# Gate and value products issued back to back in four 32-row strips, and a pipelined prologue

## The chip, the cores and the metric

The kernel runs on one core of a Trainium2 chip. The metric is the device time of one execution in microseconds (us). The kernel before takes 1056.0 us (median of two runs, 1054.63 to 1057.37).

In the profile, PE is the matmul engine, PEld its weight loads, DVE the vector engine, ACT the scalar engine, POOL the GpSimd engine and SP the engine that queues most transfers. "L267" is line 267 of the kernel that the trace belongs to. The granted clock is the share of full speed at which PE was allowed to run, by the profile. PSUM is the memory that PE writes its products to. A strip is the band of rows of PE's array that a product occupies, here 32 or 64 of 128.

## The reference, cut to what matters

Two stages follow each other. The first is attention through 32 inducing points, the second a gated feed-forward layer:

```
h    = softmax(scale * I @ x.T) @ x          # per batch, 32 x 128
x2   = softmax(scale * x @ h.T) @ h          # per token, rank 32
g, v = x2 @ w_gate, x2 @ w_val               # 128 -> 1536
out  = x2 + sigmoid(x2 @ w_res) * ((gelu(g) * v) @ w_out)
```

There are 4 batches of 12416 tokens of 128 channels. Because x2 is a mix of the 32 rows of h, the kernel never forms x2 for the wide products: it multiplies h by w_gate and w_val once per batch (`hg`, `hv`, 1536 columns) and mixes the results with the softmax weights of each token (`rt`). The contraction of the gate and value products is thus only 32 long. `h`, `hg`, `hv` and `rt` are stored four times, in partitions 0-31, 32-63, 64-95 and 96-127.

## The kernel before

A group is 512 tokens (the last group of a batch has 128). A group has six slots of 256 hidden columns, each of two 128-column chunks. Gate and value chunks use two copies at once, 64 rows, with 0.5 in the weights to make up for the doubling:

```python
def slot_mms(gi, si, weights):
    ...
    for c in [i // 2 + (i % 2) * half for i in range(2 * half)]:
        if c < cn:
            r = slice(64, 128) if c >= half else slice(0, 64)
            pe.matmul(v[:, c * tw:(c + 1) * tw],
                      weights[b][r, (c0 + c) * P:(c0 + c + 1) * P], rt[r, :],
                      start=True, stop=True)
```

The loop over slots (`prev` is the group before, whose output products `mms` fill PE's time; `gate` and `residual` are two small mixes that ACT reads with a tanh and a copy; `end` is the last multiply of a group on DVE):

```python
for p in range(nper):
    if nxt[0] < ngrp:
        gate_slot(*nxt)                 # gate products and GELU of slot p+1
    if prev and p == nper - 1:
        ...  prev.end()
    if prev:
        prev.mms(quota // 2)            # five output products
    value_mms(gi, p)                    # into the buffer that the GELU of p has read
    value_mul(gi, p)                    # DVE: u = gelu * value
    if prev:
        prev.mms(quota - quota // 2)    # five more
    if prev and p == 0:
        prev.gate()
    elif prev and p == 2:
        prev.residual()
    for f in todo.pop((g, p), []):      # work for the next batch
        f()
```

There are three PSUM buffers of 1024 columns for gate/value, shared with the scores, one for the output products and one for mixes. Work for the next batch (loading x, scores, exponentials, accumulation, `hg` and `hv`) is spread over the groups. Three bursts of exponentials per batch interrupt the plain groups. The prologue makes h of batch 0: 13 tiles of x, each transposed, copied, scored and accumulated in turn; then weights are cast, seven softmax tiles are normalised on POOL and transposed by DMA, and last w_out is loaded and scaled on DVE.

The softmax here doesn't subtract the row's maximum and nothing guards it: scores larger than these inputs give would overflow.

Of the kernel before, what the change touches and what calls it, by code (L numbers as in the profile page):

```python
# [9 lines left out]
FP32 = mybir.dt.float32  # L10
# [3 lines left out]
AC = mybir.ActivationFunctionType  # L14
# [4 lines left out]
def kernel(  # L19
# [171 lines left out]
    def first_layer(dst, w, b, c0, c1, eng):  # L191
        bank = wide_bank()
        for c in range(c0, c1, TOK):
            e = min(c + TOK, c1)
            pe.matmul(bank[:, c - c0:e - c0], ht_t[b], w[:, c:e], start=True, stop=True)
        if eng is act:
            act.activation(dst[:, c0:c1], bank[:, :c1 - c0], AC.Copy, bias=0.0, scale=0.5)
        else:
            ve.tensor_scalar(dst[:, c0:c1], bank[:, :c1 - c0], 0.5, None, op0=AL.mult)

    def res_layer(b):
        bank = misc_bank()
        pe.matmul(bank[:, :P], ht_t[b], wR, start=True, stop=True)
        hr = p_h.tile([P, P], FP16, name="hr", tag="hr")
        hr_t[b] = hr
        act.activation(hr, bank[:, :P], AC.Copy, bias=0.0, scale=1.0)

    def exp_b(b, j0, j1):
        n = (j1 - j0) * M
# [43 lines left out]

    gv_t, ge_t, u_t = {}, {}, {}

    def slot_mms(gi, si, weights):
        b, k, j0, nb, slots = groups[gi]
        tw = nb * P
        c0, cn = slots[si]
        rt = rt_t[b, k][:, j0:j0 + nb, :].rearrange("p j t -> p (j t)")  # L260
        v = gv_t[gi, si]
        half = TOK // tw

        for c in [i // 2 + (i % 2) * half for i in range(2 * half)]:
            if c < cn:
                r = slice(64, 128) if c >= half else slice(0, 64)
                pe.matmul(v[:, c * tw:(c + 1) * tw],  # L267
                          weights[b][r, (c0 + c) * P:(c0 + c + 1) * P], rt[r, :],
                          start=True, stop=True)

    def gate_slot(gi, si):
        n = groups[gi][4][si][1] * groups[gi][3] * P
        gv_t[gi, si] = wide_bank()
        slot_mms(gi, si, hg_t)
        ge = p_ge.tile([P, 2 * TOK], FP32, name="ge", tag="ge")
        act.activation(ge[:, :n], gv_t[gi, si][:, :n], AC.Gelu, bias=0.0, scale=1.0)  # L276
        ge_t[gi, si] = ge

    def value_mms(gi, si):
        slot_mms(gi, si, hv_t)  # L280

    def value_mul(gi, si):
        n = groups[gi][4][si][1] * groups[gi][3] * P
# [4 lines left out]
    class Last:  # L288
# [17 lines left out]
                pe.matmul(self.ffn[:, k, :], u_t[self.gi, si][:, o:o + P], wO[:, fc, :],  # L306
                          start=(fc == 0), stop=(fc == FCH - 1))

        def mix(self, h, r):
            bank = misc_bank()  # L310
            for k in range(self.nk):
                pe.matmul(bank[:, k * P:(k + 1) * P],  # L312
                          rt_t[self.b, self.k][r, self.j0 + k, :],
                          h[r, :], start=True, stop=True)
            return bank

        def gate(self):
            bank = self.mix(hr_t[self.b], slice(0, M))
            self.th = p_fin.tile([P, TOK], FP32, name="th", tag="th")
            act.activation(self.th[:, :self.tw], bank[:, :self.tw], AC.Tanh,  # L320
                           bias=0.0, scale=0.5)

        def residual(self):
            bank = self.mix(ha_t[self.b], slice(0, 2 * M))
            self.at = p_fin.tile([P, TOK], FP32, name="at", tag="at")
            act.activation(self.at[:, :self.tw], bank[:, :self.tw], AC.Copy,  # L326
                           bias=0.0, scale=1.0)
# [42 lines left out]
    pieces = []  # L370
    for dst, src in ((wG, moe_w_gate), (wV, moe_w_val), (wR, moe_w_res)):
        n = dst.shape[1]
        for o in range(0, n, PRE * P):
            w = min(PRE * P, n - o)
            pieces.append((dst[:, o:o + w], src[:, o:o + w], w))

    def weight_in(i):
        dst, src, w = pieces[i]
        wf = p_x.tile([P, PRE, P], FP32, name="xf", tag="xf")
        xf_t["w", i] = wf  # L380
        sy.dma_start(wf.rearrange("p k c -> p (k c)")[:, :w], src)

    def weight_cast(i, eng):
        dst, src, w = pieces[i]
        eng.tensor_copy(dst, xf_t.pop(("w", i)).rearrange("p k c -> p (k c)")[:, :w])


    for k in range(ntile):
        convert(0, k, ve, po if k % 2 else ve)
        if k + 3 < ntile:  # L390
            fetch(0, k + 3)
        elif k + 3 - ntile < len(pieces):
            weight_in(k + 3 - ntile)
        turn_pe(0, k)
        n0, w = blocks_of(k)
        exp_a(0, n0, n0 + w)
        if k:
            p0, pw = blocks_of(k - 1)
            accumulate(0, p0, p0 + pw, k == 1, False)
    n0, w = blocks_of(ntile - 1)  # L400
    for i in range(len(pieces)):
        weight_cast(i, po)
        if i + 3 < len(pieces):
            weight_in(i + 3)
    accumulate(0, n0, n0 + w, False, True)
    finish_h(0)
    turn_h(0)
    half = PRE // 2
    e2 = exp_b(0, 0, PRE)
    norm_b(0, 0, PRE, e2)  # L410
    weights_b(0, 0, 0, half)
    weights_b(0, 0, half, PRE)
    for i, c0 in enumerate(range(0, F, 2 * TOK)):
        c1 = min(c0 + 2 * TOK, F)
        first_layer(hg_t[0], wG, 0, c0, c1, act)
        first_layer(hv_t[0], wV, 0, c0, c1, ve)
    res_layer(0)
    for j0 in range(PRE, 8 * PRE, 4 * PRE):
        j1 = min(j0 + 4 * PRE, 8 * PRE)
        e2 = exp_b(0, j0, j1)  # L420
        norm_b(0, j0, j1, e2)
        for k in range(j0 // PRE, j1 // PRE):
            weights_b(0, k)
    for o in range(0, FCH, PRE):
        w = min(PRE, FCH - o)
        wf = p_x.tile([P, PRE, P], FP32, name="xf", tag="xf")
        sy.dma_start(wf[:, :w, :], moe_w_out.rearrange("(f p) d -> p f d", p=P)[:, o:o + w, :])
        ve.tensor_scalar(wO[:, o:o + w, :], wf[:, :w, :], 0.5, None, op0=AL.mult)
    warm = ps_f.tile([P, TOK // P, P], FP32, name="ffn", tag="ffn")
    for i in range(14):  # L430
        pe.matmul(warm.rearrange("p k c -> p (k c)"), wG[:, :P], wG[:, :TOK],
                  start=True, stop=True)

# [3 lines left out]
    def plan(b):  # L437
# [3 lines left out]
            todo.setdefault((g, p), []).append(f)  # L441

        nb = b + 1
        if nb < B:
            for k in range(ntile):
                g = k if k < 10 else k + 1
                at(g, 1, lambda k=k: fetch(nb, k))
                at(g + 1, 1, lambda k=k: convert(nb, k, po, po))
                at(g + 1, 4, lambda k=k: turn(nb, k))
# [13 lines left out]
        if nb < B:  # L463
            for h in range(2):
                for i in range(2):
                    j0 = (4 * h + 2 * i) * PRE
                    at(11 + h, 3 + i, lambda j0=j0, i=i: accumulate(
                        nb, j0, j0 + 2 * PRE, i == 0, i == 1))

            def burst_two():  # L470
                exp_a(nb, nfull, nblk - 1)
                exp_a(nb, nblk - 1, nblk)
            at(16, 3, burst_two)
            at(17, 3, lambda: accumulate(nb, nfull, nfull + 2 * PRE, True, False))
            at(17, 4, lambda: accumulate(nb, nfull + 2 * PRE, nblk, False, True))
            at(18, 1, lambda: finish_h(nb))
            at(18, 3, lambda: turn_h(nb))
            spots = [(18, 4), (18, 5), (19, 1), (19, 3), (19, 4)]
            for c0 in range(0, F, 2 * TOK):
                c1 = min(c0 + 2 * TOK, F)  # L480
                at(*spots.pop(0), lambda c0=c0, c1=c1: first_layer(hg_t[nb], wG, nb, c0, c1, act))
                at(*spots.pop(0), lambda c0=c0, c1=c1: first_layer(hv_t[nb], wV, nb, c0, c1, act))
            at(*spots.pop(0), lambda: res_layer(nb))

            def burst_three():
                for j0, j1 in ((0, 4 * PRE), (4 * PRE, 8 * PRE)):
                    norm_b(nb, j0, j1, exp_b(nb, j0, j1))
            at(20, 3, burst_three)
            for i in range(8):
                at(20 + (i + 2) // 3, 2 * ((i + 2) % 3), lambda i=i: weights_b(nb, i))  # L490
        return todo
# [4 lines left out]
    for gi in range(ngrp):  # L496
# [7 lines left out]
        for p in range(nper):  # L504
            nxt = (gi, p + 1) if p + 1 < nper else (gi + 1, 0)
            if nxt[0] < ngrp:
                gate_slot(*nxt)
            if prev and p == nper - 1:
                prev.mms(len(prev.todo))
                if nper == 2:  # L510
                    prev.residual()
                prev.end()
            if prev:
                prev.mms(quota // 2)
            value_mms(gi, p)
            value_mul(gi, p)
            if prev:
                prev.mms(quota - quota // 2)
            if prev and p == 0:
                prev.gate()  # L520
            elif prev and p == 2:
# [40 lines left out]
```

## Time and profile before

| | before |
|---|---|
| time, median | 1056.0 us |
| span of the profiled run | 1045.0 us |
| PE / DVE / ACT busy | 86 / 77 / 73% |
| mean granted clock of PE | 0.948 |
| interval between group ends, plain groups | 8.95 us |
| first multiply of the slots / first group end | 77.99 / 95.27 us |

The "group end" is the start of the last DVE instruction of a group (L331 in the kernel before, L333 in the changed one). Intervals between these starts show a period far better than shares of the span. The row of the page that gives the clock granted to PE in 40 equal slices of the span, in tenths:

```profile
PEclk9967998899989999899989999899998999999999
```

The 6 and 7 at the left are the idle start; the 8s lie behind the bursts.

### The profile page before, as it was taken

To read this page: it belongs to the slowest core of one execution; us is meant where nothing else is said; L and a number is where in the kernel's file an instruction comes from. 1 tells how busy PE (TensorE), PEld (TensorE's weight loads), DVE (VectorE), ACT (ScalarE), POOL (GpSimd) and SP (SyncE) were. 2 spreads that over 40 slices of the span, in tenths; PEclk is the share of its full clock that TensorE was granted. 3 is DMA by queue.
4 is the path that set the end of the run, shared out by engine and by line. 5 is a ranking of instruction groups with operands and counts; after the bars stand their busy time and mean duration, and the time that the engine had idled before them with its cause. 6 is when DMAs were issued, how large, how long until landed. Compare 5 with 4: busy or idle time off the path is not lost.

```text
span 1045.0 us, 23183 instructions
## 1 busy us (share of the span) xinstructions
PE 896.1 (86%) x9536; PEld 487.5 (47%) x9536; DVE 804.8 (77%) x776; ACT 768.0 (73%) x879; POOL 353.1 (34%) x308
## 2 busy tenths in 40 slices
PE   4618998999789899898889999898889899889997
PEld 3404444545445444444445444455444444444444
DVE  6317887787678888687777888678777888788886
ACT  4416788677867778778777877778777778887775
POOL 3452553621162554351134444441125111141111
PEclk9967998899989999899989999899998999999999
DMA  6362452510043444440022545340014000030000
GB/s 212 103 125 72 122 121 63 123 45 22 22 92 95 114 115 106 69 90 32 21 61 72 121 117 114 78 115 33 21 34 100 27 29 31 32 73 31 32 30 35
DMA packets 114186, 77.04 MB, mean 74 GB/s; under 512 B 92416, under 2 KB 95136, under 8 KB 114080
## 3 DMA queue, kind: packets, MB, share of 16 engines
q1 hardware_dynamic: 114080, 75.57, 28.7%
q8 instruction: 74, 1.21, 0.5%
q14 instruction: 32, 0.26, 0.1%
HBM read 27.87 MB, written 25.43 MB: 51 GB/s over the span
## 4 chain that ended last, share of the span: by engine, by line
PE 73%; DVE 11%; ACT 7%; issue 5%; DMA 2%; POOL 1%; SPq 0%; DVEq 0%; POOLq 0%; ACTq 0%
PE ffn L306 34%; PE gv L267 30%; PE ms L312 6%; DVE th L331 5%; DVE u L285 5%; ACT ge L276 2%; ACT xt L123 1%; PE gv L122 1%; PE gv L132 1%; DMA rt<-a 1%; ACT e L213 1%; DVE z L220 1%; PE ms L153 1%; ACT e L140 1%; POOL a L234 1%
## 5 line engine op out<-in xcount | busy, mean ns | idle before, releaser
L285 DVE TENSOR_TENSOR u<-ge,gv 128x1024 bf16<-128x1024 f32 x584 | 701.7, 1215 | 171.1 <-PE gv L267 167.9
L276 ACT ACTIVATE ge<-gv 128x1024 f32<-128x1024 f32 x584 | 593.0, 1019 | 112.4 <-PE gv L267 98.2
L306 PE MATMUL ffn<-wO,u 128*128 128x128 bf16 x4656 | 438.5, 226 | 21.4 <-DVE th L331 19.6
L306 PEld LDWEIGHTS <-u 128*128 128x128 bf16 x4656 | 276.9, 99 | 252.6 <-issue 241.2
L334 POOL TENSOR_TENSOR at<-at,th 128x512 f32<-128x512 f32 (+1 forms) x100 | 123.9, 1239 | 598.2 <-ACT ge L276 312.8
L267 PE MATMUL gv<-rt,hg 64*128 64x512 f16 (+1 forms) x1200 | 250.9, 392 | 84.2 <-DVE u L285 70.9
L267 PE MATMUL gv<-rt,hv 64*128 64x512 f16 (+1 forms) x1200 | 235.6, 392 | 9.1 <-ACT ge L276 9.1
L267 PEld LDWEIGHTS <-hg 64*128 64x128 bf16 x1200 | 77.6, 94 | 161.1 <-issue 124.5
L320 ACT ACTIVATE th<-ms 128x512 f32<-128x512 f32 (+1 forms) x100 | 58.5, 585 | 84.1 <-PE ms L312 81.8
L234 POOL TENSOR_TENSOR a<-e,z 128x1024 f16<-128x1024 f32 (+2 forms) x53 | 92.2, 1753 | 44.2 <-DVE z L221 32.0
L267 PEld LDWEIGHTS <-hv 64*128 64x128 bf16 x1200 | 66.2, 93 | 73.8 <-issue 20.8
L107 POOL TENSOR_TENSOR lo<-xf,hi 128x1024 f16<-128x1024 f32 (+1 forms) x45 | 90.8, 2018 | 19.4 <-DVE hi L105 19.0
L326 ACT ACTIVATE at<-ms 128x512 f32<-128x512 f32 (+1 forms) x100 | 58.4, 584 | 41.5 <-PE ms L312 41.5
L331 DVE SCALAR_TENSOR_TENSOR th<-th,ffn 128x512 f32<-128x512 f32 (+1 forms) x100 | 66.4, 664 | 6.1 <-ACT th L320 4.7
L312 PEld LDWEIGHTS <-rt 32*128 32x128 f16 (+1 forms) x776 | 44.7, 95 | 24.8 <-issue 5.6
L312 PE MATMUL ms<-ha,rt 64*128 64x128 f16 x388 | 39.3, 221 | 2.4 <-ACT th L320 2.4
L105 POOL CAST hi<-xf 128x1024 f16<-128x1024 f32 (+1 forms) x39 | 38.2, 981 | 8.4 <-DMA xf<-in_x_dram 8.4
L312 PE MATMUL ms<-hr,rt 32*128 32x128 f16 x388 | 40.0, 223 | 0.5 <-ACT at L326 0.5
L132 PEld LDWEIGHTS <-xt 128*128 128x128 f16 x776 | 22.8, 98 | 24.7 <-ACT xt L123 17.1
L132 PE MATMUL gv<-I1T,xt 128*128 128x32 f16 x388 | 13.7, 182 | 18.7 <-ACT xt L123 13.8
L220 DVE TENSOR_REDUCE z<-e 128x32 f32<-128x1024 f32 (+3 forms) x17 | 15.1, 887 | 13.8 <-ACT e L213 13.8
L123 ACT ACTIVATE xt<-gv 128x1024 f16<-128x1024 f16 (+1 forms) x13 | 12.6, 967 | 16.4 <-PE gv L122 16.4
(58 smaller groups left out, 237.2 us busy)
## 6 DMA issues: line engine op xcount, KB each, us to landing
xf<-in_x_dram SPq DMA_DIRECT2D x48, 512.0 KB, 4.2
out_dram<-at SPq DMA_DIRECT2D x96, 256.0 KB, 2.1
rt<-a SPq DMA_TRANSPOSE x53, 3.1
xt<-hi SPq DMA_TRANSPOSE x39, 4.5
xf<-in_moe_w_gate_dram SPq DMA_DIRECT2D x1, 512.0 KB, 3.4
xf<-in_moe_w_val_dram SPq DMA_DIRECT2D x1, 512.0 KB, 3.8
xf<-in_moe_w_out_dram SPq DMA_DIRECT2D x1, 512.0 KB, 4.5
xf<-in_x_dram SPq DMA_DIRECT2D x4, 64.0 KB, 2.1
```

The source lines that it names most:

```text
L107: e_lo.tensor_tensor(lo[:, :w, :P], xf[:, :w, :], hi[:, :w, :], AL.subtract)
L132: pe.matmul(bank[:, (j - j0) * M:(j - j0 + 1) * M], xt_t[b, k][:, jj, :], rows, start=True, stop=True)
L234: po.tensor_tensor(a2[:, :n], ev[:, o:o + n, :].unsqueeze(2).to_broadcast([P, n, Q, M]), z[:, 1, o:o + n].unsqueeze(2).unsqueeze(3).to_bro ...
L267: pe.matmul(v[:, c * tw:(c + 1) * tw], weights[b][r, (c0 + c) * P:(c0 + c + 1) * P], rt[r, :], start=True, stop=True)
L276: act.activation(ge[:, :n], gv_t[gi, si][:, :n], AC.Gelu, bias=0.0, scale=1.0)
L285: ve.tensor_tensor(u[:, :n], ge_t.pop((gi, si))[:, :n], gv_t.pop((gi, si))[:, :n], AL.mult)
L306: pe.matmul(self.ffn[:, k, :], u_t[self.gi, si][:, o:o + P], wO[:, fc, :], start=(fc == 0), stop=(fc == FCH - 1))
L312: pe.matmul(bank[:, k * P:(k + 1) * P], rt_t[self.b, self.k][r, self.j0 + k, :], h[r, :], start=True, stop=True)
L320: act.activation(self.th[:, :self.tw], bank[:, :self.tw], AC.Tanh, bias=0.0, scale=0.5)
L326: act.activation(self.at[:, :self.tw], bank[:, :self.tw], AC.Copy, bias=0.0, scale=1.0)
L331: ve.scalar_tensor_tensor(self.th[:, :tw], self.th[:, :tw], 1.0, self.ffn.rearrange("p k c -> p (k c)")[:, :tw], AL.add, AL.mult)
L334: po.tensor_tensor(self.at[:, :tw], self.at[:, :tw], self.th[:, :tw], AL.add)
```

## The change

Its intent: put all four chunks of a slot (two gate, two value) in a 32-row strip of their own, so that they can run at once; issue them together, so that PE changes between kinds of product less often; and take the serial start apart.

```diff
-                r = slice(64, 128) if c >= half else slice(0, 64)
+                r = slice((q0 + (c >= half)) * M, (q0 + (c >= half) + 1) * M)
...
-        slot_mms(gi, si, hg_t)
+        slot_mms(gi, si, hg_t, 0)
...
-        slot_mms(gi, si, hv_t)
+        slot_mms(gi, si, hv_t, 2)
...
             if nxt[0] < ngrp:
                 gate_slot(*nxt)
+            value_mms(gi, p)
             if prev and p == nper - 1:
                 ...  prev.end()
-            if prev:
-                prev.mms(quota // 2)
-            value_mms(gi, p)
             value_mul(gi, p)
             if prev:
-                prev.mms(quota - quota // 2)
+                prev.mms(quota)
```

The factor 0.5 in `hg`/`hv` becomes 1.0, and `hr` gets a low part (one small DVE subtraction per batch), so that both mixes use 64 rows. The prologue is pipelined over three tiles, its conversions are all on DVE, and weights come through ACT's queue during the first pass:

```diff
+    for k in range(ntile + 2):
+        if k < ntile:
+            convert(0, k, ve, ve)
+            ...  turn_pe(0, k)
+        if 2 <= k and k % 2 == 0 and k // 2 - 1 < len(pieces):
+            weight_in(k // 2 - 1)
+        ...
+        if 1 <= k <= ntile:
+            ...  exp_a(0, n0, n0 + w)
+        if k >= 2:
+            ...  accumulate(0, n0, n0 + w, k == 2, k == ntile + 1)
...
+        if b == 0:
+            for i in range(1, 8):
+                at((i - 1) // 2, 2 + 3 * ((i - 1) % 2), lambda i=i: weights_b(0, i))
```

Last, half of the first layer of the next batch moves into the third burst, read by DVE instead of ACT:

```diff
-            spots = [(18, 4), (18, 5), (19, 1), (19, 3), (19, 4)]
-            ...  five pieces of first layer and res_layer, on act
             def burst_three():
-                for j0, j1 in ((0, 4 * PRE), (4 * PRE, 8 * PRE)):
-                    norm_b(nb, j0, j1, exp_b(nb, j0, j1))
+                e0 = exp_b(nb, 0, 4 * PRE)
+                first_layer(hg_t[nb], wG, nb, *cs[0], ve)
+                e1 = exp_b(nb, 4 * PRE, 8 * PRE)
+                first_layer(hv_t[nb], wV, nb, *cs[0], ve)
+                norm_b(nb, 0, 4 * PRE, e0)
+                norm_b(nb, 4 * PRE, 8 * PRE, e1)
             at(20, 3, burst_three)
+            at(19, 1, lambda: first_layer(hg_t[nb], wG, nb, *cs[1], act))
+            at(19, 4, lambda: first_layer(hv_t[nb], wV, nb, *cs[1], act))
+            at(19, 3, lambda: res_layer(nb))
```

More of the change, by code (lines that the diff above doesn't have):

```diff
@@ L196, in first_layer @@
         if eng is act:
-            act.activation(dst[:, c0:c1], bank[:, :c1 - c0], AC.Copy, bias=0.0, scale=0.5)
+            act.activation(dst[:, c0:c1], bank[:, :c1 - c0], AC.Copy, bias=0.0, scale=1.0)
         else:
-            ve.tensor_scalar(dst[:, c0:c1], bank[:, :c1 - c0], 0.5, None, op0=AL.mult)
+            ve.tensor_scalar(dst[:, c0:c1], bank[:, :c1 - c0], 1.0, None, op0=AL.mult)
     def res_layer(b):
@@ L206, in res_layer @@
         act.activation(hr, bank[:, :P], AC.Copy, bias=0.0, scale=1.0)
+        ve.tensor_tensor(hr[M:2 * M, :], bank[M:2 * M, :P], hr[M:2 * M, :], AL.subtract)
     def exp_b(b, j0, j1):
@@ L254, with slot_mms @@
     gv_t, ge_t, u_t = {}, {}, {}
-    def slot_mms(gi, si, weights):
+    def slot_mms(gi, si, weights, q0):
         b, k, j0, nb, slots = groups[gi]
@@ L307, in mms, with mix @@
                           start=(fc == 0), stop=(fc == FCH - 1))
-        def mix(self, h, r):
+        def mix(self, h):
             bank = misc_bank()
+            r = slice(0, 2 * M)
             for k in range(self.nk):
@@ L317, in gate @@
         def gate(self):
-            bank = self.mix(hr_t[self.b], slice(0, M))
+            bank = self.mix(hr_t[self.b])
             self.th = p_fin.tile([P, TOK], FP32, name="th", tag="th")
@@ L323, in residual @@
         def residual(self):
-            bank = self.mix(ha_t[self.b], slice(0, 2 * M))
+            bank = self.mix(ha_t[self.b])
             self.at = p_fin.tile([P, TOK], FP32, name="at", tag="at")
@@ L372 @@
         n = dst.shape[1]
-        for o in range(0, n, PRE * P):
-            w = min(PRE * P, n - o)
-            pieces.append((dst[:, o:o + w], src[:, o:o + w], w))
-    def weight_in(i):
-        dst, src, w = pieces[i]
-        wf = p_x.tile([P, PRE, P], FP32, name="xf", tag="xf")
-        xf_t["w", i] = wf
-        sy.dma_start(wf.rearrange("p k c -> p (k c)")[:, :w], src)
-    def weight_cast(i, eng):
-        dst, src, w = pieces[i]
-        eng.tensor_copy(dst, xf_t.pop(("w", i)).rearrange("p k c -> p (k c)")[:, :w])
@@ L388 @@
-    for k in range(ntile):
-        convert(0, k, ve, po if k % 2 else ve)
-        if k + 3 < ntile:
-            fetch(0, k + 3)
-        elif k + 3 - ntile < len(pieces):
-            weight_in(k + 3 - ntile)
-        turn_pe(0, k)
-        n0, w = blocks_of(k)
-        exp_a(0, n0, n0 + w)
-        if k:
-            p0, pw = blocks_of(k - 1)
-            accumulate(0, p0, p0 + pw, k == 1, False)
-    n0, w = blocks_of(ntile - 1)
-    for i in range(len(pieces)):
-        weight_cast(i, po)
-        if i + 3 < len(pieces):
-            weight_in(i + 3)
@@ L405 @@
-    accumulate(0, n0, n0 + w, False, True)
+        for o in range(0, n, 2 * TOK):
+            w = min(2 * TOK, n - o)
+            pieces.append((dst[:, o:o + w], src[:, o:o + w], w, 1.0))
+    for o in range(0, FCH, PRE):
+        w = min(PRE, FCH - o)
+        pieces.append((wO[:, o:o + w, :].rearrange("p f d -> p (f d)"),
+                       moe_w_out.rearrange("(f p) d -> p f d", p=P)[:, o:o + w, :], w * P, 0.5))
+    staged = {}
+    def weight_in(i):
+        dst, src, w, mul = pieces[i]
+        wf = p_ge.tile([P, 2 * TOK], FP32, name="ge", tag="ge")
+        staged[i] = wf
+        v = wf[:, :w]
+        act.dma_start(v.rearrange("p (f d) -> p f d", d=P) if len(src.shape) == 3 else v, src)
@@ new lines, in weight_cast @@
+    def weight_cast(i):
+        dst, src, w, mul = pieces[i]
+        if mul == 1.0:
+            po.tensor_copy(dst, staged.pop(i)[:, :w])
+        else:
+            po.tensor_scalar(dst, staged.pop(i)[:, :w], mul, None, op0=AL.mult)
+    for k in range(ntile + 2):
+        if k < ntile:
+            convert(0, k, ve, ve)
+            if k + 3 < ntile:
+                fetch(0, k + 3)
+            turn_pe(0, k)
+        if 2 <= k and k % 2 == 0 and k // 2 - 1 < len(pieces):
+            weight_in(k // 2 - 1)
+        if 3 <= k and k % 2 and (k - 3) // 2 < len(pieces):
+            weight_cast((k - 3) // 2)
+        if 1 <= k <= ntile:
+            n0, w = blocks_of(k - 1)
+            exp_a(0, n0, n0 + w)
+        if k >= 2:
+            n0, w = blocks_of(k - 2)
+            accumulate(0, n0, n0 + w, k == 2, k == ntile + 1)
@@ L406 @@
+    weight_cast(len(pieces) - 1)
     finish_h(0)
@@ L408 @@
     half = PRE // 2
-    e2 = exp_b(0, 0, PRE)
-    norm_b(0, 0, PRE, e2)
+    norm_b(0, 0, PRE, exp_b(0, 0, PRE))
     weights_b(0, 0, 0, half)
     weights_b(0, 0, half, PRE)
+    more = [exp_b(0, j0, min(j0 + 4 * PRE, 8 * PRE)) for j0 in (PRE,)]
     for i, c0 in enumerate(range(0, F, 2 * TOK)):
@@ L417 @@
     res_layer(0)
-    for j0 in range(PRE, 8 * PRE, 4 * PRE):
-        j1 = min(j0 + 4 * PRE, 8 * PRE)
-        e2 = exp_b(0, j0, j1)
-        norm_b(0, j0, j1, e2)
-        for k in range(j0 // PRE, j1 // PRE):
-            weights_b(0, k)
-    for o in range(0, FCH, PRE):
-        w = min(PRE, FCH - o)
-        wf = p_x.tile([P, PRE, P], FP32, name="xf", tag="xf")
-        sy.dma_start(wf[:, :w, :], moe_w_out.rearrange("(f p) d -> p f d", p=P)[:, o:o + w, :])
-        ve.tensor_scalar(wO[:, o:o + w, :], wf[:, :w, :], 0.5, None, op0=AL.mult)
+    more.append(exp_b(0, 5 * PRE, 8 * PRE))
+    norm_b(0, PRE, 5 * PRE, more[0])
+    norm_b(0, 5 * PRE, 8 * PRE, more[1])
     warm = ps_f.tile([P, TOK // P, P], FP32, name="ffn", tag="ffn")
-    for i in range(14):
+    for i in range(10):
         pe.matmul(warm.rearrange("p k c -> p (k c)"), wG[:, :P], wG[:, :TOK],
@@ L477, in plan @@
             at(18, 3, lambda: turn_h(nb))
-            spots = [(18, 4), (18, 5), (19, 1), (19, 3), (19, 4)]
-            for c0 in range(0, F, 2 * TOK):
-                c1 = min(c0 + 2 * TOK, F)
-                at(*spots.pop(0), lambda c0=c0, c1=c1: first_layer(hg_t[nb], wG, nb, c0, c1, act))
-                at(*spots.pop(0), lambda c0=c0, c1=c1: first_layer(hv_t[nb], wV, nb, c0, c1, act))
-            at(*spots.pop(0), lambda: res_layer(nb))
-            def burst_three():
-                for j0, j1 in ((0, 4 * PRE), (4 * PRE, 8 * PRE)):
-                    norm_b(nb, j0, j1, exp_b(nb, j0, j1))
+            cs = [(c0, min(c0 + 2 * TOK, F)) for c0 in range(0, F, 2 * TOK)]
+            def burst_three():
+                e0 = exp_b(nb, 0, 4 * PRE)
[4 more added lines that the diff above has]
+                norm_b(nb, 4 * PRE, 8 * PRE, e1)
             at(20, 3, burst_three)
+            at(19, 1, lambda: first_layer(hg_t[nb], wG, nb, *cs[1], act))
+            at(19, 4, lambda: first_layer(hv_t[nb], wV, nb, *cs[1], act))
+            at(19, 3, lambda: res_layer(nb))
             for i in range(8):
```

## The prediction

> **What bounds the kernel now.** I read the busy shares and the shares of the chain first, then the totals of waits, then the chain inside one ordinary group of tokens, then the start of the program. A group is 512 tokens with six slots; a slot is 256 of the 1536 hidden columns: gate products (L267, hg), GELU on ACT (L276), value products into the same PSUM buffer (L267, hv), the multiply on DVE (L285). Between them PE runs the 48 output products (L306) of the group before; L331 on DVE and the two mixes (L312, read by ACT in L320 and L326) occur once per group.
>
> ```profile
> PE 896.1 (86%) x9536; PEld 487.5 (47%) x9536; DVE 804.8 (77%) x776; ACT 768.0 (73%) x879; POOL 353.1 (34%) x308
> PE 73%; DVE 11%; ACT 7%; issue 5%; DMA 2%; POOL 1%; SPq 0%; DVEq 0%; POOLq 0%; ACTq 0%
> DVE u L285 <- PE gv L267: 167.9, 375, 3.6
> PE gv L267 <- DVE u L285: 70.9, 88, 22.1
> ```
>
> The first line is busy time, the second the chain's shares: PE carries it. The last two are waits (total us, times, longest): DVE waits for products 375 times, PE for DVE only 88 times, one of which lasts 22.1 us and belongs to the start. The starts of L331 lie 8.95 us apart in all undisturbed groups. The chain of one of them:
>
> ```profile
> 404.37 0.69 DVE th L331
> ...
> 407.28 0.32 PE gv L267 x2
> 407.60 0.39 PE ffn L306 x5
> 407.99 0.32 PE gv L267 x2
> 408.31 0.39 PE ffn L306 x5
> ...
> 412.34 0.56 PE gv L267 x4
> ...
> 413.32 0.69 DVE th L331
> ```
>
> Two 512-column products in two 64-row strips take 0.32 us, five output products 0.39. The x4 line is two pairs with no burst between them: 0.56, so the second pair cost 0.24. About 0.1 us of each pair, and likewise of each burst, is therefore the change of kind. A slot is 2 x (0.32 + 0.39) = 1.42 us of PE; its multiply is 1.22 us of DVE (1.17 back to back), its GELU 1.02 us of ACT. So PE is the bound, but DVE is only 15% behind it.
>
> The start is a separate loss:
>
> ```profile
> 43.03 0.43 DVE L160 COPY nacc<-ms 128x257 f32<-128x257 f32 x1 [8.64 <-PE ms L155]
> 55.90 0.39 PE L267 MATMUL gv<-rt,hv 64*128 64x512 f16 x2 [0.90 <-ACT ge L276]
> 76.83 1.25 DVE L428 TENSOR_SCALAR wO<-xf 128x1024 bf16<-128x1024 f32 x2 [22.15 <-DMA xf<-in_moe_w_out_dram]
> ```
>
> The first pass over x ends at 43.03, the value products of slot 0 are there at 55.90, but DVE stands in order behind the scaling of w_out, whose transfer was queued behind seven transposes each waiting for POOL. The first multiply begins at 77.99, PE has meanwhile been idle, and its granted clock is 0.63 from 78 to 95 us. Groups of 13.2 to 13.5 us appear six times later, after the exponential bursts: there the clock was 0.50 (289 to 298 us).
>
> **What the Trainium skill says.** "TensorEngine Tiling (Array Packing)", section Key Properties: changing the tiling mode drains TensorE, and different tiles can run in parallel. The trace agrees: the pair of strips takes hardly more than one product, and the 0.32 against 0.24 above is the change of kind. "TensorE: Matmul & The Clock Gate", Part 3, gives 3.07x for four K=32, N=512 row strips; no instruction of this trace has that form, so I take concurrency of four as likely, not shown. Its Part 1 says an idle TensorE falls back to half clock; 0.50 after idle stretches agrees. "SBUF — State Buffer", section Who interferes with whom: DVE casts in a two-port mode and GpSimd block each other. The trace agrees: the cast L105 takes 0.69 us, but up to 2.65 where POOL's L107 runs beside it, in the prologue that the change takes L107 on POOL out of.
>
> **The change, part by part.**
>
> *Products.* Gate of slot p+1 and value of slot p are issued together, each chunk in one of four 32-row strips, and the ten output products follow as one burst. If the strips overlap, a quad costs at best 0.32 instead of 0.64, and the long burst 10 x 0.056 + 0.11 = 0.67 instead of 0.78. PE's need per slot falls from 1.42 to about 0.99, so six slots and mixes need about 6.5 us of 8.95. This is not the gain, because other chains take over.
>
> DVE per group: 6 x 1.17 + 0.60 (L331 to the next multiply) = 7.6 us. ACT: 6 x 0.97 + 2 x 0.5 = 6.8. But engines run in order, and a value product now stands directly behind the next gate, with no burst to fill the wait for its GELU. I follow the even slots, where the mixes sit, with latencies of this trace:
>
> ```profile
> 406.18 0.39 PE L312 MATMUL ms<-hr,rt 32*128 32x128 f16 x4
> 406.67 0.60 ACT L320 ACTIVATE th<-ms 128x512 f32<-128x512 f32 x1 [0.71 <-PE ms L312]
> 407.16 1.02 ACT L276 ACTIVATE ge<-gv 128x1024 f32<-128x1024 f32 x1
> ```
>
> Mix to tanh 0.49, tanh to the GELU behind it 0.49; GELU to its value product 1.02 + 0.08 = 1.10. Slot 0: value to mix 0.32 + 0.67, then 0.49 + 0.49, so GELU 2 starts 1.97 later; plus 1.10 to value 2. Slot 2: the same with 0.44 for the residual mix, 1.92 + 1.10. Slot 4 has eight output products and no mix: 0.32 + 0.56 to the next gate, 0.43 from gate to GELU (404.50 to 404.93), 1.10. Sum 3.07 + 3.02 + 2.41 = **8.5 us per group**, the longest loop I find. (Three PSUM buffers give (0.43 + 1.10 + 0.50 + 1.22 + 0.05) / 3 = 1.10 us a slot, shorter.) So 0.45 us per group, 95 groups after the first L331: **43 us**. In the six half-clock groups the loop is about 11.2 instead of 13.3, 1.6 beyond the 0.45: **9 us**.
>
> *First layer of the next batch.* Two of four wide evictions per batch move from ACT between slots to DVE inside the third exponential burst, where DVE stood idle 1.66 us. Two ACT pieces of 1.02 leave, two DVE pieces of 1.22 come, partly beside the exponentials: 1 us per batch, three batches, **3 us**.
>
> *hr.* One small subtraction per batch, and the gate mix at 64 instead of 32 rows: both mixes take the same time now (223 against 221 ns); nothing.
>
> *Prologue.* A tile takes 3.04 us now because transpose, copy, scores and accumulation follow each other. Software pipelining leaves DVE 0.69 + 1.23 = 1.92 and the input loop (4.4 us from issue to landing, plus the conversion, over three buffers) about 2.1; with 2.4 MB of weights alongside I take 2.5. That ends the first pass about 6 us sooner. The chain from there to the value products of slot 0 stays, 12.9 us. The 22 us behind w_out go, as it is loaded during the first pass and seven POOL/transposition steps move into groups 0 to 3. First multiply: 43.0 - 6 + 12.9 + 0.5 = 50.4 instead of 77.99. Then six slots without output products (7.2) and one full group (8.5): first L331 at about **66.5** instead of 95.3, a gain of 29 us, some of it from a clock that no longer falls. POOL then carries 2 x 1.90 + 1.04 + 2.13 + 1.27 = 8.2 us a group in groups 0 to 3: tight, but under 8.5.
>
> Sum: 66.5 + (1045 - 95.3) - 43 - 9 - 3 = 961 us of span. Timed executions were 1056.0 against a span of 1045.0, a factor of 1.0105: **970 us**.
>
> **Rivals.** (1) *DVE is the only new bound.* If PE and ACT chains hide, a group is 7.6 to 8.0 us: another 0.5 to 0.9 a group, about 905 to 920. For it: 375 waits of DVE for products. Against: the loop above, and only one misc PSUM buffer. (2) *The filler is missed.* The burst between gate and value covered the GELU wait; if PE now waits in every slot and strips don't overlap (quad 0.56), the even loop gains 0.24 on up to three steps and a group is back near 8.95 to 9.1: only the start is won, about 1010 to 1020. (3) *The clock falls more often.* PE gets more short gaps; a group at half clock is about 11.2, so one group in four cold would add some 60 us. Against: gaps stay well under 1 us, and the dips now come after bursts with longer gaps. (4) *The prologue gain is given back:* POOL overloaded in groups 0 to 3 delays transposes and token groups by a few us each, at most about 12.
>
> **Range and chances.** The start alone gives 2.8%, and it rests on a plainly visible stall. Group period between 8.15 and 8.85 is worth -33 to +33 us, the prologue +-5. Range 935 to 1005. Faster by over 2% 0.95, within 2% 0.04, slower 0.01.
>
> **What will show it right or wrong.** L331 starts 8.5 us apart in plain groups, mixes and tanh followed by late GELUs in even slots; first L331 near 66; no 22 us wait of DVE for w_out; four L267 products with starts within tens of ns where the GELU was done; PE busy well under 86%, DVE above 77% but not full. It is wrong if the period is 8.0 (DVE back to back) or 8.9 (strips don't overlap), or if the clock line shows new dips.

## The result, and the profile after

The changed kernel takes 983.0 us (median of two runs, 982.05 to 984.01). Its ratio to the kernel before is 0.9309, 95% interval 0.9244 to 0.9374. Here and below a ratio is the mean time of one kernel's fast runs over the mean of the other's fast runs of the same rounds, so it is not quite the ratio of the medians quoted. Executions over 1.5% slower than the fastest of the same kernel are left out of the means. All outputs are right. The span of the profiled run is 980.3 us.

The page of the changed kernel: the busy shares, the clock row, and three totals of waits (us, times, longest us). L286 is the multiply (285 before), L277 the GELU (276), L268 the gate and value products (267).

```profile
PE 810.8 (83%) x9532; PEld 480.8 (49%) x9532; DVE 809.1 (83%) x790; ACT 739.0 (75%) x873; POOL 344.4 (35%) x304
PEclk9678998979888997988887998898979798999998
DVE u L286 <- PE gv L268: 87.2, 206, 3.0
PE gv L268 <- ACT ge L277: 75.6, 225, 1.4
PE gv L268 <- DVE u L286: 43.9, 85, 2.0
```

DVE's waits for products have halved, and a new wait stands beside them: PE now waits 225 times for a GELU (12 times before), because the value products stand directly behind the next gate pair. The clock row has many more 7s and 8s than before: the mean fell from 0.948 to 0.892. That is the surprise of this page, and it is not in the shares.

In plain groups the interval fell from 8.95 to 8.40 us. But of the 56 intervals that took about 8.95 us before, lie apart from the bursts and should now be 8.40, 12 stand out with 8.76 to 10.34 us. In 11 of them the granted clock was 0.66 to 0.82; in the one of 8.76 us it was 1.00, so that one has another cause. Two neighbours in the table of stretches (start and end, length; then busy us with the number of instructions for PE, PEld, DVE, ACT and POOL; last the granted clock, the DMA share and GB/s):

```profile
95.63:104.89 9.26, 8.33 (x80) 5.01 (x80) 7.75 (x9) 6.90 (x9) 4.45 (x4) 0.82 0.48 128
104.89:113.29 8.40, 7.09 (x80) 4.04 (x80) 7.65 (x8) 6.79 (x9) 4.45 (x4) 1.00 0.49 126
```

Both run the same 80 products. In the first the granted clock was 0.82, PE was busy 1.24 us longer, and the interval grew by 0.86 us. Before, a single plain interval was longer by more than 0.1 us (9.31).

Here is the second of these groups in order of time. Each line is start, duration, engine, line, what it writes and reads; I left out the odd slots and the output products.

```profile
105.63 0.39 PE L268 MATMUL gv<-rt,hv 32*128 32x512 f16 x2 [0.22 <-ACT ge L277]
...
106.62 0.39 PE L314 MATMUL ms<-hr,rt 64*128 64x128 f16 x4
...
106.95 0.39 PE L268 MATMUL gv<-rt,hg 32*128 32x512 f16 x2
106.95 0.39 PE L268 MATMUL gv<-rt,hv 32*128 32x512 f16 x2
...
107.11 0.60 ACT L322 ACTIVATE th<-ms 128x512 f32<-128x512 f32 x1 [0.62 <-PE ms L314]
...
107.61 1.94 ACT L277 ACTIVATE ge<-gv 128x1024 f32<-128x1024 f32 x2
...
108.67 0.39 PE L268 MATMUL gv<-rt,hv 32*128 32x512 f16 x2 [0.35 <-ACT ge L277]
...
109.66 0.39 PE L314 MATMUL ms<-ha,rt 64*128 64x128 f16 x4
...
110.09 0.60 ACT L328 ACTIVATE at<-ms 128x512 f32<-128x512 f32 x1 [0.55 <-PE ms L314]
...
110.59 1.94 ACT L277 ACTIVATE ge<-gv 128x1024 f32<-128x1024 f32 x2
...
111.66 0.39 PE L268 MATMUL gv<-rt,hv 32*128 32x512 f16 x2 [0.29 <-ACT ge L277]
```

The four strips do run at once: at 106.95 the gate pair and the value pair start together, and the output products behind them start at 107.27, 0.32 us later, as after one pair before. But in the even slots the value pair starts alone, when its GELU is done. Reading down the starts: value to mix 0.99, mix to tanh 0.49, tanh to GELU 0.50, GELU to value 1.06, and again 0.99, 0.43, 0.50, 1.07. From the value pair at 111.66 it is 0.87 to the next group's gate pair (112.53), 0.43 to its GELU (112.96) and about 1.07 to its value pair. The sum is 8.40 us, the interval itself. The period is set by this loop and by no engine's work: DVE is busy 7.65 us of it.

Three lines show the start: the end of the first pass, the first multiply, and a DVE conversion that waited for x.

```profile
39.64 0.43 DVE L160 COPY nacc<-ms 128x257 f32<-128x257 f32 x1 [2.09 <-PE ms L155]
53.78 3.48 DVE L286 TENSOR_TENSOR u<-ge,gv 128x1024 bf16<-128x1024 f32 x3 [2.12 <-PE gv L268]
19.17 1.40 DVE L105 CAST hi<-xf 128x1024 f16<-128x1024 f32 x1 [4.27 <-DMA xf<-in_x_dram]
```

The wait of 22 us for w_out is gone; the first multiply comes at 53.78 instead of 77.99. The first pass is only 3.4 us shorter than before: DVE waited 4.27 us once for x while the first weights were in flight beside it for 8.5 us (that they were the cause is likely, not tested), and a tile's eight transposes still took 1.03 us almost to the end of it (0.62 in one tile near 30 us).

The 64.7 us between the two spans (the medians lie 73 us apart, because the profiled execution of the kernel before was a fast one) divide as follows, by the intervals between group ends (sums in us):

| part | before | after | difference |
|---|---|---|---|
| up to the first group end | 95.3 | 69.8 | -25.5 |
| 60 intervals of about 8.95 us before | 537.5 | 515.8 | -21.7 |
| 11 intervals at batch ends (128-token group) | 73.6 | 77.4 | +3.8 |
| 28 intervals with bursts, first layer, and clock recovery | 335.1 | 313.5 | -21.7 |
| behind the last group end | 3.5 | 3.9 | +0.4 |

The batch ends became slower, and the plain groups gained less than 60 x 0.55 = 33 us. Both follow the clock, as the run `two_strips` will show. For the stretch from 70 to 976 us the mean clock is 0.90. The clock's own record in the trace holds only the values 1 and 0.5, and half clock adds up to 181 us of this stretch. Before, from the first group end on, the mean was 0.96, with 75 us at half clock.

### The profile page after: what moved, and what is told of

Read it like the earlier page. It is cut to its first block, busy times and chain, and to the rows that moved or that the text cites. A ratio compares the mean times of both kernels' runs of the same rounds, so it can differ in the third digit from the quotient of the medians.

```text
span 980.3 us, 23172 instructions
## 1 busy us (share of the span) xinstructions
PE 810.8 (83%) x9532; PEld 480.8 (49%) x9532; DVE 809.1 (83%) x790; ACT 739.0 (75%) x873; POOL 344.4 (35%) x304
## 5 line engine op out<-in xcount | busy, mean ns | idle before, releaser
L286 DVE TENSOR_TENSOR u<-ge,gv 128x1024 bf16<-128x1024 f32 x584 | 695.4, 1214 | 122.3 <-PE gv L268 87.2
L277 ACT ACTIVATE ge<-gv 128x1024 f32<-128x1024 f32 x584 | 571.9, 1020 | 72.0 <-PE gv L268 71.4
L307 PE MATMUL ffn<-wO,u 128*128 128x128 bf16 x4656 | 381.5, 235 | 0.2
L307 PEld LDWEIGHTS <-u 128*128 128x128 bf16 x4656 | 292.3, 105 | 126.4 <-issue 124.4
L268 PE MATMUL gv<-rt,hv 32*128 32x512 f16 (+1 forms) x1200 | 248.9, 409 | 77.0 <-ACT ge L277 75.6
L268 PE MATMUL gv<-rt,hg 32*128 32x512 f16 (+1 forms) x1200 | 245.4, 410 | 55.6 <-DVE u L286 43.9
L268 PEld LDWEIGHTS <-hv 32*128 32x128 bf16 x1200 | 84.2, 92 | 156.9 <-issue 154.9
L268 PEld LDWEIGHTS <-hg 32*128 32x128 bf16 x1200 | 62.6, 92 | 143.9 <-issue 101.1
L107 POOL TENSOR_TENSOR lo<-xf,hi 128x1024 f16<-128x1024 f32 (+1 forms) x39 | 78.0, 2001 | 0.4
L314 PEld LDWEIGHTS <-rt 64*128 64x128 f16 x776 | 48.1, 100 | 26.6 <-issue 10.2
L314 PE MATMUL ms<-hr,rt 64*128 64x128 f16 x388 | 44.8, 244 | 0.7 <-ACT at L328 0.7
```

The costliest lines, as they stand in the source:

```text
L107: e_lo.tensor_tensor(lo[:, :w, :P], xf[:, :w, :], hi[:, :w, :], AL.subtract)
L268: pe.matmul(v[:, c * tw:(c + 1) * tw], weights[b][r, (c0 + c) * P:(c0 + c + 1) * P], rt[r, :], start=True, stop=True)
L277: act.activation(ge[:, :n], gv_t[gi, si][:, :n], AC.Gelu, bias=0.0, scale=1.0)
L286: ve.tensor_tensor(u[:, :n], ge_t.pop((gi, si))[:, :n], gv_t.pop((gi, si))[:, :n], AL.mult)
L307: pe.matmul(self.ffn[:, k, :], u_t[self.gi, si][:, o:o + P], wO[:, fc, :], start=(fc == 0), stop=(fc == FCH - 1))
L314: pe.matmul(bank[:, k * P:(k + 1) * P], rt_t[self.b, self.k][r, self.j0 + k, :], h[r, :], start=True, stop=True)
```

## The experiments

The theory after the result had four parts. The start and the products are separate gains that add up. The loop through the mix sets the plain group. The move of the first layer is a loss, not a gain. And the more frequent half clock comes from the change of the products. The rival for the last two: the four strips are what gains, and the clock is an accident of PE being less busy.

### The start alone, and the products alone

`prologue_only` is the kernel before with the prologue of the changed one, and nothing else. `products_only` is the kernel before with the strips, the new order, the factor 1.0 and the wide `hr`; its prologue and first-layer places are the old ones. The diffs are the corresponding parts of the change above.

> The kernel before with the new prologue alone (64-row strips, old order of products, first-layer evictions where they were). Theory: the start is worth 24 to 29 us and nothing of it is given back, so about 1028 us, first L331-type multiply near 70 us, later groups 8.95 us as before. Rival: transposition work moved into groups 0 to 3 overloads POOL and gives back 10 us or more: 1040 us, with groups 1 to 7 longer than 8.95.

> The kernel before with the 32-row strips, the new order of products and the wide hr alone. Theory: plain groups 8.40 us as in the changed kernel, 45 to 50 us won there, some 10 us given back through more half-clock stretches: about 1010 us. If the gains of start and products do not add up, it is below 1000 or above 1020.

| kernel | time, us | ratio to before (95%) | plain interval | first group end |
|---|---|---|---|---|
| prologue_only | 1023.4 | 0.9762 (0.9699 to 0.9826) | 8.95 | 69.0 |
| products_only | 997.2 | 0.9494 (0.9445 to 0.9543) | 8.40 | 94.6 |

The start alone gave what was expected, and groups 1 to 8 stayed at exactly 8.95 us, so POOL gave nothing back. The products did better than expected, and 997.2 us is even below the 1000 that the expectation had named as a sign that the gains don't add up. The ratios say that they do: their product is 0.9268, and the kernel that contains both without the first-layer move (`old_layer`, next) measured 0.9244.

### The first layer back in its old place

```diff
-            at(19, 1, lambda: first_layer(hg_t[nb], wG, nb, *cs[1], act))   # and the rest of the move
+            spots = [(18, 4), (18, 5), (19, 1), (19, 3), (19, 4)]
+            ...  as in the kernel before, all on act
```

> The changed kernel with the first-layer evictions of the next batch back where they were (ACT, between slots of groups 18 and 19). The prediction gave the move a gain of 1 us per batch: then 986 us. Rival: the group with the third burst grew from 13.35 to 17.1 us because DVE evictions and normalisation now stand in one row there; if that outweighs what groups 18 and 19 won, this kernel is faster, 975 to 980 us.

It took 970.5 us, ratio 0.9244 (0.9189 to 0.9299). The interval of this ratio overlaps that of the changed kernel, so the timing alone doesn't settle the 12 us between the medians. The traces show part of it in one place: the interval with the third burst and the one ahead of it take 8.83 + 17.07 us in the changed kernel and 10.75 + 12.89 in this one, 2.25 us per batch, 7 us in three batches. Here is the changed kernel's third burst in order of time:

```profile
246.14 1.22 DVE L199 TENSOR_SCALAR hg<-gv 128x1024 bf16<-128x1024 f32 x1 [0.68 <-PE gv L195]
...
247.41 0.95 PE L132 MATMUL gv<-ht,xt 128*128 128x32 f16 x32 [1.31 <-DVE hg L199]
...
248.84 1.23 DVE L199 TENSOR_SCALAR hv<-gv 128x1024 bf16<-128x1024 f32 x1 [1.48 <-PE gv L195]
...
249.99 1.21 DVE L221 TENSOR_REDUCE z<-e 128x32 f32<-128x1024 f32 x1
...
252.96 1.16 DVE L286 TENSOR_TENSOR u<-ge,gv 128x1024 bf16<-128x1024 f32 x1
```

Only two PSUM buffers turn there, since slot 4 holds the third. So the scores at 247.41 wait 1.31 us for DVE to empty hg's buffer, and the normalisation, which stands behind hv in DVE's order, begins at 249.99, though its exponentials were done at 247.64 (a start of 246.62 plus 1.02). The next multiply comes at 252.96.

### The changed order with two 64-row strips

```diff
-                r = slice((q0 + (c >= half)) * M, (q0 + (c >= half) + 1) * M)
+                r = slice(64, 128) if c >= half else slice(0, 64)      # and scale 0.5 again
```

> The changed kernel with its order, but gate and value both in the two 64-row strips (scale 0.5 again), so that the value pair can't run beside the gate pair. Theory (the loop through mix, tanh, GELU and value sets the group, and in even slots the value products wait for their GELU anyway): plain groups 8.4 to 8.6 us, 983 to 1000 us. Rival (the four strips at once are the source of the gain): plain groups about 8.9, 1020 us or more.

It took 959.8 us, ratio 0.9139 (0.9093 to 0.9184): **faster** than the changed kernel, and the two intervals do not overlap. Undisturbed plain groups take 8.41 us against 8.40. So the four strips bring nothing at full clock, as the loop above requires: in even slots the value pair waits for its GELU anyway. What differs is the clock. Here are the kernel before, the changed one and this one behind the first group end:

```profile
95.30:1041.00 945.70, 845.87 (x8949) 458.60 (x8949) 760.80 (x722) 730.40 (x831) 315.22 (x263) 0.96 0.27 68
70.00:976.00 906.00, 765.98 (x8952) 452.24 (x8950) 762.54 (x730) 702.81 (x825) 322.39 (x267) 0.90 0.29 72
70.00:955.00 885.00, 766.02 (x8945) 442.36 (x8942) 759.49 (x729) 701.01 (x824) 321.84 (x267) 0.96 0.29 74
```

The mean clock is 0.96 again, and 2 of the 56 plain intervals stand out, against 12 (one of the two, again 8.76 us, at full clock). The two sums that the clock had spoilt become 506.8 (plain) and 71.0 us (batch ends), 9.0 and 6.4 us less than in the changed kernel.

### The strips under the old order, and the same with 64 rows

`burst_between` puts half of the output products between gate and value again and keeps the four 32-row strips; `between_64` is the same kernel with 64-row strips.

```diff
-            value_mms(gi, p)                       # burst_between, against the changed kernel
             if prev and p == nper - 1:
                 ...
+            if prev:
+                prev.mms(quota // 2)
+            value_mms(gi, p)
             value_mul(gi, p)
             if prev:
-                prev.mms(quota)
+                prev.mms(quota - quota // 2)
```

> The changed kernel with its four 32-row strips, but half of the output products between gate and value again, as before. If the new order is what gains (fewer changes of kind, 0.1 us each, two per slot): plain groups near 8.9 us, about 1025 us. If the strips by themselves gain: below 8.6 us, under 1000 us.

> The slow kernel burst_between with one thing changed back: gate and value in two 64-row strips (scale 0.5). If the rows in use decide the granted clock: clock about 0.94 instead of 0.54, plain groups 8.95 us instead of 13.77, about 1020 to 1035 us. If it is the order of that kernel: it stays at half clock, above 1400 us.

Neither expectation for `burst_between` came near: 1413.8 us (median of its two fast runs; all four lie between 1407.8 and 1442.1), ratio 1.3465 (1.3327 to 1.3602), with a mean clock of 0.543. `between_64` took 1009.2 us, ratio 0.9617 (0.9576 to 0.9658), with a clock of 0.944. The stretch from 90 to 140 us, first of `burst_between`:

```profile
90.00:140.00 50.00, 48.78 (x295) 22.54 (x292) 27.67 (x25) 25.60 (x29) 19.93 (x17) 0.50 0.39 95
```

and of `between_64`:

```profile
90.00:140.00 50.00, 45.51 (x450) 24.31 (x449) 43.66 (x40) 40.35 (x46) 24.26 (x21) 1.00 0.54 130
```

In the first, PE was busy for 48.78 of 50 us, and still its clock stayed at one half; the plain interval is 13.77 us. In the second it was busy for less time, at full clock, and did half as many products again. The two kernels differ in the rows of the gate and value products alone (and the factor that goes with them). So a clock of one half does not need idle gaps to last, and the 32-row strips bring it about. Together with `two_strips` this names the cause of the dips, and my prediction's argument, that gaps would stay short, did not touch it.

### Every gate pair twice

```diff
         slot_mms(gi, si, hg_t, 0)
+        slot_mms(gi, si, hg_t, 0)
```

> The changed kernel with every gate pair issued twice to the same place (same result), about 0.22 us more PE work per slot. Theory of the clock (the more frequent half-clock stretches come from PE being less busy than before, and PE has slack): the granted clock rises from 0.89 to 0.93 or more, the plain group grows by no more than 0.25 us, time within 10 us of 983. If PE has no slack: plain groups 8.4 + 6 x 0.22 = 9.7 us, 1090 us. If the clock does not follow how busy PE is: clock stays 0.89.

It took 1018.3 us, ratio 0.9699 (0.9642 to 0.9756). The undisturbed plain interval is 8.67 us, 0.27 more than in the changed kernel (0.25 at most was expected) although 1.3 us of products were added, so PE has slack there. Only 3 of the 56 plain intervals stand out (12 in the changed kernel), and the stretch from 105 to 139 us has a clock of 1.00: with more products in the array, the plain groups keep their clock. But the time was 35 us above the changed kernel's and the mean clock rose only to 0.91, not to 0.93: groups behind the bursts, which were at half clock anyway, now had more to do (up to 14.7 us). As a remedy it is useless; as a sign of what the clock follows it agrees with the run before.

### Each mix before the output products, and each mix between gate and value

`mix_ahead` issues the mix ahead of the ten output products. `mix_fill` issues it between the gate pair and the value pair, where PE waits for the GELU:

```diff
             if nxt[0] < ngrp:
                 gate_slot(*nxt)
+            if prev and p == 0:
+                prev.gate()
+            elif prev and p == 2:
+                prev.residual()
             value_mms(gi, p)
             ...
-            if prev and p == 0:
-                prev.gate()
-            elif prev and p == 2:
-                prev.residual()
```

> The changed kernel with each mix issued before the ten output products instead of behind them. Theory (mix, tanh or copy, then the GELU of the next slot in ACT's order is the link that sets 8.40 us): the link shortens by about 0.2 us twice per group, plain groups about 8.0 us, 945 to 965 us. Rival (DVE or PE alone sets the group): no change, 8.4 us, 983 us.

> The changed kernel with each mix issued between the gate pair and the value pair, where PE waits for the GELU anyway. Theory: the loop through the mix falls below DVE's need of 7.6 us (six multiplies and one L333), so plain groups 7.7 to 8.0 us, 930 to 955 us. Rival: mix apart from the loop, no change, or slower because the quad is torn apart: 983 us or more.

| kernel | time, us | ratio to before (95%) | undisturbed plain interval |
|---|---|---|---|
| mix_ahead | 958.1 | 0.9090 (0.9003 to 0.9177) | 8.02 |
| mix_fill | 936.1 (its three fast runs) | 0.8912 (0.8843 to 0.8981) | 7.77 |

Both periods came out as the loop said, 8.0 and 7.7 to 8.0 us, from moving two mixes of four small products each. The lines of `mix_fill` show the link that has gone:

```profile
124.30 0.39 PE L314 MATMUL ms<-hr,rt 64*128 64x128 f16 x4
124.63 0.39 PE L268 MATMUL gv<-rt,hv 32*128 32x512 f16 x2
125.34 0.60 ACT L322 ACTIVATE th<-ms 128x512 f32<-128x512 f32 x1
126.14 2.15 ACT L277 ACTIVATE ge<-gv 128x1024 f32<-128x1024 f32 x2 [0.20 <-PE gv L268]
```

The mix stands ahead of the value pair, and the GELU at 126.14 waits for its own gate products, no longer for the tanh, which is done at 125.94. The loop through the mix is therefore shown. In `mix_ahead` 23 of the 56 plain intervals take some 9.05 us (mean clock 0.883), so part of its gain is lost to the half clock; in `mix_fill` only 4 stand out. (Why so many in `mix_ahead` is taken up below.)

### The parts that help, put together

`fill_32_old` is `mix_fill` with the first layer in its old place; `fill_64_old` has 64-row strips as well; `fill_64_new` has 64-row strips and the first layer where the change put it.

> mix_fill (each mix between gate and value, 937.6 us) with the first-layer evictions of the next batch back in groups 18 and 19 on ACT. If the loss of the move (12 us between the changed kernel and old_layer) adds up with the mix: about 925 us. If the third burst is hidden now: 937 us.

> fill_32_old with gate and value in two 64-row strips as well: order of products and prologue of the change kept, strips and first-layer placement taken back, mixes moved. If the half-clock stretches in plain groups go as in two_strips and the four strips give nothing at full clock: plain groups 7.8 us, 905 to 920 us, clock 0.94 or more. If the four strips at once matter now that PE has less slack: plain groups above 8.0 us, no better than fill_32_old.

> fill_64_old with the first-layer evictions where the change put them (half on DVE inside the third burst, half on ACT in group 19). If the move costs what groups 18 and 19 showed between the changed kernel and old_layer (2.25 us per batch, three batches) it is about 900 us; if it costs nothing beside the mixes between gate and value, as fill_32_old against mix_fill suggests, 893 us.

| kernel | time, us | ratio to before (95%) | plain interval |
|---|---|---|---|
| fill_32_old | 935.5 | 0.8912 (0.8882 to 0.8942) | 7.77 |
| fill_64_old | 892.7 | 0.8506 (0.8466 to 0.8546) | 7.64 |
| fill_64_new | 893.6 | 0.8500 (0.8435 to 0.8566) | 7.64 |

Taking the strips back is worth 43 us here (935.5 to 892.7), more than expected (905 to 920). The place of the first layer is worth nothing beside `mix_fill`, with 32 or with 64 rows (936.1 and 935.5; 893.6 and 892.7): the loss seen in `old_layer` belongs to the changed kernel and is not a rule. Here is DVE in `fill_64_old`:

```profile
118.62 0.68 DVE L333 SCALAR_TENSOR_TENSOR th<-th,ffn 128x512 f32<-128x512 f32 x1
119.22 7.12 DVE L286 TENSOR_TENSOR u<-ge,gv 128x1024 bf16<-128x1024 f32 x6
126.25 0.68 DVE L333 SCALAR_TENSOR_TENSOR th<-th,ffn 128x512 f32<-128x512 f32 x1
```

Six multiplies and the group end follow each other without a gap: 7.63 us. DVE is the bound of the plain group at last, and a further gain there would have to take work from DVE. This kernel beats both: 892.7 us against 983.0 of the changed and 1056.0 of the kernel before.

## Why the prediction was right or wrong

It said 970 us, 935 to 1005; measured were 983.0. Range and direction held, but one of its own signs of being wrong came true: "if the clock line shows new dips". That the number came so near is partly luck. The last factor, 1.0105, set the time of one execution against the span of another, faster one; a run's time is only 1.8 us above its own span. The 961 us of span thus meant 963 us, 20 below the measured time and not 13. By its steps:

- **PE stops being the bound of a plain group, and the loop through mix, tanh, GELU and value takes over at 8.5 us.** Right: 8.40 us, and each link of the sum is within 0.04 us of what was written down (GELU to value 1.06 instead of 1.10 makes most of the difference). `mix_ahead` and `mix_fill` show that it is this loop.
- **Four strips overlap, but that is not the gain.** Right, and more so than written: `two_strips` has the same period without them.
- **The six half-clock groups, 9 us.** Misread in part: of the six intervals of 13.2 to 13.5 us, the three behind the first burst of a batch had a clock of 0.69 or 0.70 and did shrink to 11.0 to 11.2. But the three of 13.35 us are groups with the third burst, at 0.97; with the first layer moved into them they grew to 17.1 or 17.2.
- **Prologue 29 us.** The measured part up to the first group end is 25.5 us. The mis-sized term is the first pass, put at 6 us and measured at 3.4 (43.03 to 39.64); the chain from there to the value products of slot 0, put at 12.9, took 13.64. The other steps held: the 22 us wait went, and POOL gave nothing back.
- **First layer, 3 us gained.** Wrong in the changed kernel: the step "DVE stood idle 1.66 us" counted DVE's idle time and not the PSUM buffers and DVE's order behind it. Read from the two intervals it cost 2.25 us per batch. Beside `mix_fill` the move cost nothing and gained nothing.
- **Rival 3, the clock falls more often.** This is the step that failed. It was set aside with "gaps stay well under 1 us", and the sum has no term for it. The gaps did stay short (0.47 us at the longest in the 3.4 us ahead of the fall at 96.5 us), and the clock fell all the same. Behind the first group end, 55 us were to be won; the changed kernel won 39, and `two_strips`, the same order with 64 rows, won 59. The difference lies in the plain groups (60 x 0.45 = 27 us forecast, 21.7 won) and at the batch ends (11 x 0.45 = 5 us forecast, 3.8 lost). Rival 3 did come true in part, but by another cause than gaps: rows.
- **Rival 1, DVE as the only new bound**, was rightly put aside for this change; it becomes true in `fill_64_old`. **Rival 2**, a group back near 9 us, did not occur. **Rival 4**, gains of the start given back, did not occur.

The experiments show that 32-row strips bring the clock down and that more products per time can bring it back (`gate_twice`, `mix_fill`). They do not say whether the active rows count or the 32-row form as such, nor why `mix_ahead`, with a shorter period than the changed kernel, had more dips. A count over the kept traces answers both. In every trace the clock changes only at whole steps of 3.41 us. For each step between the first and the last group end, the products that start in it are added up as rows x columns x moved columns, in units of one output product (128 x 128 x 128): a 32-row gate or value product is 1 unit, a 64-row one is 2.

| clock in a step | units in it | steps | clock in the next step |
|---|---|---|---|
| full | 24 or more | 2716 | full in 2698 |
| full | under 24 | 244 | half in 229 |
| half | under 24 | 546 | half in 532 |
| half | 24 or more | 258 | full in 234 |

One threshold fits all 14 kernels, with 32-row and 64-row strips, in 98% of the steps. The same count without rows fits 90% at best, PE's busy share 83%, and always guessing full clock 79%. So the clock follows the amount of work in these traces, with rows counted, and not the 32-row form. A count is no test, and the 24 units are an estimate from it, but it agrees with the runs that are tests. A plain group of the changed kernel is 76 units in 8.40 us, a mean of 31 per step, so a thin step can fall short: from 93.10 to 96.51 us it had 10 output and 12 gate and value products, 22 units, and the clock fell at 96.5, though PE was busy for 2.44 of the 3.41 us. With 64 rows a group is 100 units, a mean of 41. `burst_between`, once at half clock, does 76 units in 13.77 us, 19 per step, and stays there. And in `mix_ahead` a group of 8.02 and one of 9.05 us make exactly five steps (17.07 us), so the same thin stretch meets a step in every second group. What the count can't tell is whether columns matter as rows do: without columns it fits as well.

## What to carry to other kernels

Narrower strips that run at once are worth something only if PE's time is on the chain; check first whether the products wait for each other's inputs. Compare the granted clock of a kernel before and after such a change in plain stretches, because a kernel can lose there what its order gains; in the count above a 32-row product holds the clock half as well as a 64-row one. And where an in-order engine takes a small product for another engine, issue it in a spot where its own engine waits anyway: moving two mixes per group was worth more than the strips.

## What the Trainium skill lacked or had wrong

- "TensorE: Matmul & The Clock Gate", Part 1, says that the clock follows how busy PE has been, and warns of idle gaps. It lacks that narrow strips count for less, and how much work holds the clock (in these traces about 24 products of 128 x 128 x 128 per 3.41 us): with 32-row gate and value strips PE was busy 48.78 of 50 us and its granted clock was 0.50; with 64-row strips it was busy 45.51 us and the clock 1.00. Its Part 3 and closing table recommend 32-row packing without this caution. Here the four strips did start together, yet the kernel with them was 23 us slower than the same order with two 64-row strips (983.0 against 959.8 us).
- "TensorEngine Tiling (Array Packing)", section Key Properties, says that a change of mode drains TensorE, but gives no figure. In the trace of the kernel before, a pair followed by another pair took 0.24 us and one followed by output products 0.32, so a change cost about 0.1 us.
